# Exponentials by shifted bit patterns, PV by query halves, packed heads and free score slots in an attention and MLP kernel

## The chip, the cores and the metric

The kernel runs on one core of one Trainium2 chip. The metric is the device time of one execution in microseconds; lower is better. A run of a one-core program is called fast when it lies within 1.5% of the fastest run of the same kernel; unless it is said otherwise all numbers are from fast runs. A profile is of one execution and its span is some 2 us shorter than that execution's time. The clock that is given beside a run is TensorE's granted clock, as a share of full speed, averaged over the run.

## The reference

```python
# A: attention over 2048 tokens, 32 heads of 16;  B: token-mixing MLP with 1376 hidden units
xn = layernorm(x)                                   # x: [1, 2048, 512], bf16
q, k, v = split(xn @ wqkv)                          # 32 heads, Dh = 16
p = softmax(q @ k.T * 16 ** -0.5)                   # [32, 2048, 2048]: 134 million exponentials
A = concat(p @ v) @ wo
B = (gelu(layernorm(xn).T @ w1 + b1) @ w2 + b2).T
return x + A + B
```

## The kernel before

Scores (Q times K) are made transposed, keys on partitions; PV is the product of their exponentials with V. TensorE's results land in PSUM (`ps` in the profile), of which the kernel uses eight banks. One unit of work n is 128 keys by 512 queries of two heads, a tile of 128x1024; there are 1024 of them. Two score matmuls with 32 contracted rows each fill the tile's two PSUM banks. Three pairs of banks are score slots; one bank collects PV, one serves all else (projections, the MLP, the out-projection). A matmul is written for a split of TensorE's array, its tiling mode: score matmuls use 32 rows by 128 columns (32*128 in the profile), PV uses 128 rows by 32 columns (128*32), a column tile, and up to four column tiles work side by side (in the trace four PV matmuls of 128x512 start within 0.03 us of each other at 221.79 us, and the next four matmuls at 222.01). A scheduler written in Python goes through the program at build time with its own guesses of durations and fixes the order on every engine.

ScalarE turns most tiles into `exp` with one instruction. VectorE does some of them, with integer arithmetic on bf16 bit patterns, in five instructions. Score tiles go to the slot `n % 3`.

```python
def pslot(n):
    return n % 2 if n < 2 * NKT else n % 3

def exp_specs(n):                                   # ScalarE
    ... e.activation(pT[:, pbuf[n], :], ps[:, s_ * 1024:(s_ + 1) * 1024], ACTF.Exp, scale=LN2_128)

def d_specs(n, buf):                                # VectorE
    dW_i = max(ps + IBIAS, 0)                       # from PSUM; int16 that is read as bf16
    dM_i = (dW_i & 0x7f) | 0x3f80                   # the mantissa
    dA_i = dW_i & -128                              # the exponent alone
    dM   = dM * dM
    dM   = dW * dM                                  # exp ~ V.dW + V.dA + (171/1024 V).dM
    # (written here as formulas; each line is one VectorE instruction)

def pv_specs(item, first, last):
    for i in range(2):                              # two heads, two of four column tiles
        r = 2 * (n % 2) + i
        ... e.matmul(bank(PV_BANK)[32 * r:32 * r + 32, :], lhsT=vt[:, off:off + 32],
                     rhs=tile[:, buf, 512 * i:512 * (i + 1)], tile_position=(0, 32 * r))
# ... cut: the two head pairs' PV steps are emitted together when both are ready
# a tile goes to VectorE when the last one was 4 tiles ago and its backlog is under 1.6 us
```

V carries a column of 0.5, so that PV also gives the softmax's denominators. The head outputs stand in PSUM at 16 of each 32 rows, and the out-projection contracts 128 such rows of which half are empty (`wo_pad` holds zeros there): eight steps for each output tile.

The softmax here doesn't subtract the row's maximum and nothing guards it: scores larger than these inputs give would overflow.

## Time and profile before

| | before |
|---|---|
| time, median of the first 3 runs | 812.09 us (810.02 to 819.36) |
| ScalarE exponentials | 824 |
| VectorE exponentials | 200 |
| mean granted TensorE clock | 0.978 |

The first line is the page's busy time by engine (us, share of the span, instructions). PE is TensorE, PEld its weight loads, DVE VectorE, ACT ScalarE, POOL GpSimd.

```profile
PE 754.5 (93%) x8184; PEld 230.1 (28%) x8184; DVE 764.3 (94%) x1304; ACT 771.7 (95%) x845; POOL 76.8 (9%) x88
```

The windows view gives busy us of each engine in stretches of the span, then the granted TensorE clock as a share of full speed.

```profile
core 0: us, PE busy (x) PEld busy (x) DVE busy (x) ACT busy (x) POOL busy (x), PEclk, DMA share, GB/s
200.00:300.00 100.00, 99.11 (x1136) 27.67 (x1128) 97.95 (x164) 99.83 (x114) 0.00 (x0) 1.00 0.23 48
300.00:400.00 100.00, 97.03 (x898) 26.24 (x894) 92.27 (x153) 99.56 (x109) 0.00 (x0) 0.98 0.11 25
400.00:500.00 100.00, 94.82 (x998) 27.31 (x998) 96.31 (x161) 98.78 (x108) 0.00 (x0) 0.99 0.12 29
500.00:600.00 100.00, 91.00 (x708) 25.93 (x704) 99.11 (x166) 99.26 (x109) 0.00 (x0) 1.00 0.06 11
600.00:700.00 100.00, 95.62 (x998) 27.61 (x994) 96.38 (x162) 100.00 (x110) 0.00 (x0) 1.00 0.12 29
```

Three engines are full at once in the long middle part, and GpSimd does nothing there. So no single engine can be relieved by giving its work to another of the three.

The costliest groups of instructions: source line, engine, output and input, shapes, count, busy us and mean ns, idle time before them.

```profile
L606 ACT ACTIVATE pT<-ps 128x1024 bf16<-128x1024 f32 x824 | 763.2, 1113 | 15.4 <-PE ps L590 14.6
...
L617 DVE TENSOR_SCALAR dW<-ps 128x1024 int16<-128x1024 f32 x200 | 243.4, 1217 | 23.0 <-PE ps L590 21.9
...
L506 POOL TENSOR_SCALAR VM<-V 128x544 bf16<-128x544 bf16 x16 | 29.0, 1811 | 47.6 <-DVE V L739 42.1
```

A mean duration is no cost: successive instructions overlap (VectorE's pass over PSUM below lasts 1.23 us, and the next one starts after 1.14). What one costs an engine that is full is the step from its start to the next start. In VectorE's timeline (start us, duration us):

```profile
400.92 1.23 DVE L617 TENSOR_SCALAR dW<-ps 128x1024 int16<-128x1024 f32 x1 [1.01 <-PE ps L590]
...
402.06 0.68 DVE L628 TENSOR_TENSOR dM<-dW,dM 128x1024 bf16<-128x1024 bf16 x1
...
402.66 0.42 DVE L620 TENSOR_SCALAR dM<-dW 128x1024 int16<-128x1024 int16 x1
...
402.99 0.42 DVE L623 TENSOR_SCALAR dA<-dW 128x1024 int16<-128x1024 int16 x1
...
403.33 0.68 DVE L626 TENSOR_TENSOR dM<-dM 128x1024 bf16<-128x1024 bf16 x1
...
403.93 0.24 DVE L835 RECIPROCAL rcomp<-dcomp 128x16 f32<-128x16 f32 x1
```

The steps are 1.14, 0.60, 0.33, 0.34 and 0.60 us, together 3.01 us for one exponential. For ScalarE the chain of waits has a piece of 18 in a row, 16.61 / 18 = 0.923 us each:

```profile
402.43 16.61 ACT pT L606 x18
```

824 x 0.923 = 761 us: nearly all that ScalarE does.

### The profile page before, as it was taken

The page shows a single profiled execution, that of the slowest core. Times are in us where ns is not written, and L with a number is a line of the kernel's source. Part 1 is how long each engine was busy: PE and PEld are TensorE (multiplying, and loading weights), DVE is VectorE, ACT ScalarE, POOL GpSimd, SP SyncE. Part 2 cuts the span into 40 slices and gives each one's busy share as a digit, 9 for nine tenths or more (in the row PEclk, how much of TensorE's full clock was granted, in tenths as well). Part 3 has the DMA queues.
Part 4 walks back from the last instruction along what each step waited for, and adds up shares of the span by engine and source line. Part 5 has one row for each costly group of instructions (what it writes and reads, how often), then busy time and mean ns, then how long its engine had stood idle before and what let it go on. Part 6 is the DMA issues. An engine that isn't in the chain of part 4 may idle for free.

```text
span 813.6 us, 19375 instructions
## 1 busy us (share of the span) xinstructions
PE 754.5 (93%) x8184; PEld 230.1 (28%) x8184; DVE 764.3 (94%) x1304; ACT 771.7 (95%) x845; POOL 76.8 (9%) x88
## 2 busy tenths in 40 slices
PE   5988999999999999999999999899899999999995
PEld 3532333233222222222222222222222222222221
DVE  6879999999999988999899999999999999799985
ACT  4998999999999999999999999999999999899991
POOL 5579432000000000000000000000000000000000
PEclk9999999999999999999899999999999999799998
DMA  6040000222221212100001111000001111010010
GB/s 181 2 80 15 10 16 3 42 43 58 60 55 33 46 36 50 32 22 15 4 8 37 33 48 23 16 8 6 11 8 32 40 38 34 7 27 9 8 26 27
DMA packets 73239, 25.38 MB, mean 31 GB/s; under 512 B 63104, under 2 KB 71168, under 8 KB 73152
## 3 DMA queue, kind: packets, MB, share of 16 engines
q1 hardware_dynamic: 69984, 22.57, 12.5%
q10 hardware_dynamic: 3168, 1.57, 0.7%
q8 instruction: 64, 1.05, 0.5%
q14 instruction: 23, 0.19, 0.1%
HBM read 19.54 MB, written 2.35 MB: 27 GB/s over the span
## 4 chain that ended last, share of the span: by engine, by line
ACT 43%; DVE 31%; PE 24%; DMA 1%; issue 1%; SPq 0%; DVEq 0%
ACT pT L606 42%; DVE dW L617 10%; PE ps L590 9%; PE ps L652 7%; PE ps L681 7%; DVE dM L626 5%; DVE dM L628 4%; DVE dM L620 3%; DVE dA L623 2%; DVE OT L829 1%; DVE V L739 1%; DVE KT L720 1%; DMA x_sb<-in_A_x_dram 1%; DVE oT L844 1%; PE ps L478 0%
## 5 line engine op out<-in xcount | busy, mean ns | idle before, releaser
L606 ACT ACTIVATE pT<-ps 128x1024 bf16<-128x1024 f32 x824 | 763.2, 1113 | 15.4 <-PE ps L590 14.6
L590 PE MATMUL ps<-QT,KT 32*128 32x512 bf16 x2048 | 331.5, 390 | 23.3 <-ACT pT L606 10.7
L652 PE MATMUL ps<-pT,V 128*32 128x512 bf16 x1648 | 259.0, 393 | 7.2 <-DVE OT L829 3.3
L617 DVE TENSOR_SCALAR dW<-ps 128x1024 int16<-128x1024 f32 x200 | 243.4, 1217 | 23.0 <-PE ps L590 21.9
L590 PEld LDWEIGHTS ps<-QT,KT 32*128 32x128 bf16 x2048 | 85.1, 91 | 314.1 <-ACT pT L606 121.5
L628 DVE TENSOR_TENSOR dM<-dW,dM 128x1024 bf16<-128x1024 bf16 x200 | 137.0, 685 | 1.7
L626 DVE TENSOR_TENSOR dM<-dM 128x1024 bf16<-128x1024 bf16 x200 | 137.6, 688 | 0.0
L652 PEld LDWEIGHTS ps<-pT,V 128*32 128x32 bf16 x1648 | 62.6, 94 | 99.4 <-issue 69.6
L620 DVE TENSOR_SCALAR dM<-dW 128x1024 int16<-128x1024 int16 x200 | 86.5, 433 | 1.6
L652 PE MATMUL ps<-dW,V 128*32 128x512 bf16 x400 | 79.0, 393 | 7.2 <-DVE OT L829 7.1
L623 DVE TENSOR_SCALAR dA<-dW 128x1024 int16<-128x1024 int16 x200 | 85.0, 425 | 0.0
L652 PE MATMUL ps<-dM,VM 128*32 128x512 bf16 x400 | 77.0, 389 | 1.7 <-POOL VM L506 1.3
L652 PE MATMUL ps<-dA,V 128*32 128x512 bf16 x400 | 77.6, 391 | 0.1
L681 PE MATMUL ps<-hx,wblk 128*32 128x512 bf16 x688 | 56.0, 382 | 0.0
L681 PE MATMUL ps<-wo_pad,oT 128*32 128x512 bf16 x480 | 40.0, 382 | 0.0
L681 PE MATMUL ps<-wkv_raw,wblk 128*32 128x512 bf16 x512 | 39.2, 382 | 0.2 <-DVE osb L816 0.2
L506 POOL TENSOR_SCALAR VM<-V 128x544 bf16<-128x544 bf16 x16 | 29.0, 1811 | 47.6 <-DVE V L739 42.1
L652 PEld LDWEIGHTS ps<-dW,V 128*32 128x32 bf16 x400 | 19.3, 94 | 36.4 <-issue 21.5
L453 POOL TENSOR_SCALAR hx<-hx,mv 128x512 bf16<-128x512 bf16 x16 | 26.7, 1686 | 0.1
L652 PEld LDWEIGHTS ps<-dM,VM 128*32 128x32 bf16 x400 | 19.1, 94 | 23.9 <-issue 10.7
L652 PEld LDWEIGHTS ps<-dA,V 128*32 128x32 bf16 x400 | 19.4, 95 | 20.7 <-issue 9.7
L829 DVE COPY OT<-ps 128x512 f32<-128x512 f32 x31 | 21.2, 683 | 1.1 <-PE ps L652 0.7
(79 smaller groups left out, 353.7 us busy)
## 6 DMA issues: line engine op xcount, KB each, us to landing
wblk<-in_B_w_dram SPq DMA_DIRECT2D x10, 512.0 KB, 4.5
wblk<-in_B_w_dram SPq DMA_DIRECT2D x16, 320.0 KB, 3.5
denb<-rden_scratch SPq DMA_DIRECT2D x124, 32.0 KB, 1.9
out_dram<-osb SPq DMA_DIRECT2D x16, 128.0 KB, 1.7
dcomp<-OT SPq DMA_DIRECT2D x124, 2.0 KB, 1.7
QT<-Qall SPq DMA_DIRECT2D x120, 16.0 KB, 1.8
x_sb<-in_A_x_dram SPq DMA_DIRECT2D x3, 512.0 KB, 10.3
wkv_raw<-in_A_wqkv_dram ACTq DMA_DIRECT2D x2, 384.0 KB, 8.7
```

The lines of the kernel that those rows point to most:

```text
L453: sc.add("pool", lambda e: e.tensor_scalar(xn_sb[:, t, :], xn_sb[:, t, :], mv[:, t, 3:4], None, ALU.mult), reads=[("xn", t), ("mv", t)], w ...
L506: sc.add("pool", lambda e: e.tensor_scalar(vm_kh[:, t0_:t0_ + n, 8 * T:8 * T + 8, :], v17_kh[:, t0_:t0_ + n, 8 * T:8 * T + 8, :], CM, None ...
L590: specs.append(dict(eng="pe", fn=lambda e, r=r, bk=bk: e.matmul(bank(bk), lhsT=KT[32 * r:32 * r + 32, T, 128 * kt:128 * (kt + 1)], rhs=QT[ ...
L606: return [dict(eng="act", fn=lambda e: e.activation(pT[:, pbuf[n], :], ps[:, s_ * 1024:(s_ + 1) * 1024], ACTF.Exp, scale=LN2_128), reads=[ ...
L617: yield dict(eng="dve", fn=lambda e: e.tensor_scalar(dW_i[:, buf, :], ps[:, s_ * 1024:(s_ + 1) * 1024], IBIAS, 0.0, ALU.add, ALU.max), rea ...
L620: yield dict(eng="dve", fn=lambda e: e.tensor_scalar(dM_i[:, buf, :], dW_i[:, buf, :], 0x7f, 0x3f80, ALU.bitwise_and, ALU.bitwise_or), rea ...
L623: yield dict(eng="dve", fn=lambda e: e.tensor_scalar(dA_i[:, buf, :], dW_i[:, buf, :], -128, None, ALU.bitwise_and), reads=[("dW", buf)], ...
L626: yield dict(eng="dve", fn=lambda e: e.tensor_tensor(dM[:, buf, :], dM[:, buf, :], dM[:, buf, :], ALU.mult), reads=[("dM", buf)], writes=[ ...
L628: yield dict(eng="dve", fn=lambda e: e.tensor_tensor(dM[:, buf, :], dW[:, buf, :], dM[:, buf, :], ALU.mult), reads=[("dW", buf), ("dM", bu ...
L652: specs.append(dict(eng="pe", fn=lambda e, r=r, off=off, i=i: e.matmul(bank(PV_BANK)[32 * r:32 * r + 32, :], lhsT=vt[:, off:off + 32], rhs ...
L681: specs.append(dict(eng="pe", fn=lambda e, c=c, w=w: e.matmul(bank(EX_BANK)[32 * c:32 * c + w, :], lhsT=lhs_of(32 * c, 32 * c + w), rhs=rh ...
L829: yield "pvev", [dict(eng="dve", fn=lambda e: e.tensor_copy(OT32[:, eb, :], bank(PV_BANK)), reads=[("bank", PV_BANK)], writes=[("OT32", eb)])]
```

## The change

The intent is to move exponentials from ScalarE to VectorE, by making VectorE's cheaper, and to give TensorE room for the extra PV terms.

1. The VectorE exponential is now a sum of four piecewise-linear powers of two: the bit pattern W and three copies with an integer added (22, 58, 94). Three passes of SBUF to SBUF replace four, none of them with two inputs, and GpSimd takes about a third of them.
2. One PV step covers one head pair in four column tiles, two heads by two halves of 256 queries, so it never needs a partner.
3. The heads are packed by DMA, so the out-projection needs four steps in place of eight, and the final product goes to GpSimd.
4. A score tile goes to the slot that comes free first; ScalarE or VectorE takes any tile that is ready.
5. GpSimd's single-scalar instructions get a second scalar of 1.0.

```diff
-CM = 171.0 / 1024.0
-KAPPA = 2.16705
+SHIFTS = (22, 58, 94)
+CM = 13.0 / 16.0
+KAPPA = 5.0415723
-NPB = 10
-NDB = 3
+NPB = 20
+NXB = 8                       # x_sb is reused for probability buffers
@@ VectorE exponential (dm, dA, dm2, dM removed)
+        def shift_spec(eng, w, o, k):
+            return dict(eng=eng, fn=lambda e: e.tensor_scalar(
+                buf_i(o), buf_i(w), float(SHIFTS[k]), 1.0, ALU.add, ALU.mult), ...
+                cost=(SH_I, SH_L) if eng == "pool" else (TS_I, TS_L))
@@ PV
-            for i in range(2):
-                r = 2 * (n % 2) + i
-                    bank(PV_BANK)[32 * r:32 * r + 32, :], ... rhs=tile[:, buf, 512 * i:512 * (i + 1)]
+            for c in range(4):
+                h, i = divmod(c, 2)
+                    bank(PV_BANK)[32 * c:32 * c + 32, 256 * par:256 * par + 256], ...
+                    rhs=buf(p, 512 * i + 256 * h, 512 * i + 256 * h + 256)
@@ epilogue: 8 DMAs of 16x256 pack each block's heads; product on GpSimd
-            yield "dve", [dict(eng="dve", fn=lambda e: e.tensor_tensor(oT[:, qb % 2, G, :], OT32[...], denb[...], ALU.mult)
+            yield "pool", [dict(eng="pool", fn=lambda e, cs=cs: e.tensor_tensor(oT[0:m, qb % 2, T, cs], oC32[...], denb[...], ALU.mult)
@@ slots
-            s_ = pslot(n)
+                s_ = min(free_slots, key=slot_time)
@@ which tile goes to VectorE
-                if n - last_d >= D_GAP and n % BN <= D_LAST and free_d and backlog <= D_BACKLOG:
+            if ready_q and fly < D_FLY and len(free_p) >= 4 + P_KEEP:      # and backlog(t) <= D_BACK = 0.5
@@ ... cut: the scheduler keeps GpSimd's instructions apart in time from some of VectorE's; reloading x for the residual, the tail
```

## The prediction

> **What bounds the kernel now.** In the windows view, 200 to 700 us, ScalarE is busy 98.8 to 100%, VectorE 92 to 99%, TensorE 91 to 99%: three engines are full together. ScalarE does 824 of the 1024 exponentials of 128x1024. The chain of waits runs 18 of them in 16.61 us (402 to 419 us), 0.923 us each, so 761 of ScalarE's 772 busy us. Its other 42 us are mostly prologue (18 us idle before 160 us) and tail (17 us in the last 34). VectorE does 200 exponentials in five instructions; start to start in the timeline 1.14 + 0.33 + 0.34 + 0.60 + 0.60 = 3.01 us, so 602 us, plus about 160 us of other work. TensorE pays about 0.33 us for a score run with its change of tiling mode, 0.33 us for the first step of another run, 0.22 us per further step. When only one head pair of a PV step is ready, two of four column tiles work.
>
> **What the change does (counts from the built program's instruction order).**
> - Exponentials: VectorE 200 -> 266, ScalarE 824 -> 758.
> - A VectorE exponential is one 1.14 us PSUM pass and three integer shifts (798: 527 on VectorE at 0.335 us, the trace's step for the int16 tensor_scalar, 271 on GpSimd). VectorE: 266 x 1.14 + 527 x 0.335 = 480 us instead of 602; the oT product (31 x 0.60) leaves too. Load about 620 us.
> - GpSimd: no trace has this shift. [...] The trace's one-scalar form takes 1.65 us for 544 elements, so this rests on the second scalar. [...] The shifts fit under the PSUM pass.
> - PV: 1424 two-tile steps of 512 columns become 1822 four-tile steps of 256. The trace's four-tile matmuls of 128 columns step at 56 ns per group, so 107 ns for 256 is safe.
> - Out-projection: 480 -> 240 matmuls, 13 us less.
> - Score runs 771 -> 636, others 769 -> 634: 270 mode changes of 0.11 us go. TensorE, estimated: 636 x 0.33 + 634 x 0.11 + 1475 x 0.215 = 597 us, plus score pairs that don't coincide: clear of saturation.
> - 248 DMAs of 16 KB are added, off the path.
>
> **On the critical path.** VectorE loses about 140 us, TensorE gets slack, so ScalarE alone binds: 66 x 0.923 = 61 us less, 812 - 61 = 751. I add 4 us for ScalarE idling where the static order misjudges GpSimd or clock-throttled stretches (at 400 us matmuls step at half speed).
>
> **Predicted: 755 us, range 742 to 779.** Faster by over 2%: 0.94, within 2%: 0.04, slower: 0.02.
>
> **Would show it right.** ScalarE about 706 us busy, still 98% between 200 and 700 us; exp interval 0.92 us; VectorE at 80 to 88% of the span, GpSimd about 40%; shifts of 0.42 us (VectorE) and about 1.05 us (GpSimd); TensorE at or under 90%; the chain's ScalarE share up from 43% to over 60%.
>
> **Would make it wrong.** GpSimd shifts of 1.5 us or more, or VectorE shifts stretched behind GpSimd, so PV waits for late shift buffers and score slots stay full; a granted clock that falls because four column tiles now work; ScalarE idle above 60 us because scores come late; a longer tail from the DMA packing.

Cut from the GpSimd item are its estimate of one shift and a reason for contention with VectorE, as no trace or run shows what they rested on. The estimate came to 1.07 us a shift, 290 us for 271; of its two terms only 0.19 us was read from a trace, and it is "this" in "this rests on the second scalar". "The shifts fit under the PSUM pass", "about 1.05 us" and "about 40%" for GpSimd were forecasts that came of it; the result below measures them.

## The result

| | before | changed |
|---|---|---|
| median time | 811.48 us (4 runs, 810.02 to 819.36) | 752.63 us (4 runs, 750.77 to 753.34) |
| exponentials, ScalarE / VectorE | 824 / 200 | 758 / 266 |
| mean granted clock in the profile | 0.978 | 0.968 |

The ratio is 0.924 (95% interval 0.919 to 0.929). A ratio is the mean time of one kernel's fast runs over that of the other's of the same rounds, so it isn't quite the ratio of the medians. The page's first line, then windows and groups of the changed kernel:

```profile
PE 691.1 (92%) x12388; PEld 306.2 (41%) x12388; DVE 644.6 (86%) x1061; ACT 710.8 (95%) x779; POOL 351.5 (47%) x391
```

```profile
core 0: us, PE busy (x) PEld busy (x) DVE busy (x) ACT busy (x) POOL busy (x), PEclk, DMA share, GB/s
200.00:300.00 100.00, 96.95 (x1758) 43.11 (x1754) 88.94 (x140) 100.00 (x113) 39.55 (x39) 1.00 0.25 57
300.00:400.00 100.00, 92.14 (x1586) 39.06 (x1582) 89.99 (x146) 99.25 (x109) 47.83 (x48) 0.98 0.13 31
400.00:500.00 100.00, 95.17 (x1646) 39.40 (x1644) 92.17 (x147) 100.00 (x110) 47.71 (x49) 0.98 0.18 43
500.00:600.00 100.00, 91.97 (x1546) 38.14 (x1544) 85.32 (x137) 95.11 (x104) 48.66 (x48) 0.91 0.11 25
600.00:700.00 100.00, 94.92 (x1660) 40.83 (x1656) 90.94 (x145) 97.81 (x108) 50.00 (x49) 0.97 0.17 40
```

```profile
L640 ACT ACTIVATE pT<-ps 128x1024 bf16<-128x1024 f32 x529 | 527.2, 1142 | 10.4 <-PE ps L616 9.7
...
L651 DVE TENSOR_SCALAR pT<-ps 128x1024 int16<-128x1024 f32 x197 | 240.4, 1220 | 42.7 <-PE ps L616 41.4
...
L656 POOL TENSOR_SCALAR pT<-pT 128x1024 int16<-128x1024 int16 x137 | 143.5, 1047 | 175.6 <-DVE pT L656 125.1
```

ScalarE is still full, VectorE is not. ScalarE's busy time fell by 771.7 - 710.8 = 60.9 us and the profiled span by 813.6 - 750.4 = 63.2 us; what ScalarE leaves idle in the span went from 41.9 to 39.6 us. (By its span, the profiled execution of the kernel before was longer than the median one; the medians differ by 58.9 us.) One exponential still costs ScalarE 0.92 us: the chain of waits has four in 3.68 us.

```profile
700.85 3.68 ACT x_sb L640 x4
```

In the timeline GpSimd's shift (1.05 us) lies under VectorE's PSUM pass (1.23 us), which leaves VectorE 1.14 + 2 x 0.335 us for this exponential:

```profile
402.77 1.05 POOL L656 TENSOR_SCALAR pT<-pT 128x1024 int16<-128x1024 int16 x1 [0.62 <-DVE pT L656]
402.83 1.23 DVE L651 TENSOR_SCALAR x_sb<-ps 128x1024 int16<-128x1024 f32 x1
...
403.97 0.42 DVE L656 TENSOR_SCALAR pT<-pT 128x1024 int16<-128x1024 int16 x1
...
404.31 0.42 DVE L656 TENSOR_SCALAR pT<-x_sb 128x1024 int16<-128x1024 int16 x1
...
404.64 1.22 DVE L651 TENSOR_SCALAR pT<-ps 128x1024 int16<-128x1024 f32 x1
```

### The profile page after: what moved, and what is told of

It is laid out like the page before. It is cut to its first block, busy times and chain, and to the rows that moved or that the text cites. A ratio compares the mean times of both kernels' runs of the same rounds, so it can differ in the third digit from the quotient of the medians.

```text
span 750.4 us, 28208 instructions
## 1 busy us (share of the span) xinstructions
PE 691.1 (92%) x12388; PEld 306.2 (41%) x12388; DVE 644.6 (86%) x1061; ACT 710.8 (95%) x779; POOL 351.5 (47%) x391
## 4 chain that ended last, share of the span: by engine, by line
ACT 41%; PE 31%; DVE 20%; POOL 3%; issue 2%; SPq 2%; DMA 0%; DVEq 0%; POOLq 0%
ACT pT L640 29%; PE ps L679 13%; ACT x_sb L640 12%; PE ps L616 11%; DVE pT L651 7%; PE ps L709 7%; DVE pT L656 5%; DVE x_sb L651 3%; SPq L371 2%; DVE OT L863 2%; DVE x_sb L656 1%; POOL pT L656 1%; POOL x_sb L656 1%; PE ps L758 1%; DVE denb L928 0%
## 5 line engine op out<-in xcount | busy, mean ns | idle before, releaser
L640 ACT ACTIVATE pT<-ps 128x1024 bf16<-128x1024 f32 x529 | 527.2, 1142 | 10.4 <-PE ps L616 9.7
L651 DVE TENSOR_SCALAR pT<-ps 128x1024 int16<-128x1024 f32 x197 | 240.4, 1220 | 42.7 <-PE ps L616 41.4
L679 PE MATMUL ps<-pT,V 128*32 128x256 bf16 x4456 | 243.7, 282 | 13.6 <-DVE OT L863 7.0
L640 ACT ACTIVATE x_sb<-ps 128x1024 bf16<-128x1024 f32 x229 | 248.4, 1153 | 1.9 <-PE ps L616 1.9
L656 POOL TENSOR_SCALAR pT<-pT 128x1024 int16<-128x1024 int16 x137 | 143.5, 1047 | 175.6 <-DVE pT L656 125.1
L679 PE MATMUL ps<-x_sb,V 128*32 128x256 bf16 x1768 | 117.5, 282 | 9.0 <-DVE OT L863 6.3
L656 DVE TENSOR_SCALAR pT<-pT 128x1024 int16<-128x1024 int16 x288 | 120.8, 445 | 2.6
L656 POOL TENSOR_SCALAR x_sb<-pT 128x1024 int16<-128x1024 int16 x64 | 67.0, 1046 | 66.9 <-DVE pT L656 50.1
L651 DVE TENSOR_SCALAR x_sb<-ps 128x1024 int16<-128x1024 f32 x69 | 84.2, 1220 | 16.0 <-PE ps L616 15.4
L656 POOL TENSOR_SCALAR pT<-x_sb 128x1024 int16<-128x1024 int16 x53 | 55.4, 1046 | 63.2 <-DVE pT L656 46.1
L679 PE MATMUL ps<-pT,VM 128*32 128x256 bf16 x772 | 55.6, 278 | 0.4 <-POOL VM L531 0.3
```

What stands on the lines that cost most here:

```text
L640: return [dict(eng="act", fn=lambda e: e.activation(buf(pbuf[n]), ps[:, s_ * 1024:(s_ + 1) * 1024], ACTF.Exp, scale=LN2_128), reads=[("ban ...
L651: return dict(eng="dve", fn=lambda e: e.tensor_scalar(buf_i(w), ps[:, s_ * 1024:(s_ + 1) * 1024], IBIAS, 0.0, ALU.add, ALU.max), reads=[(" ...
L656: return dict(eng=eng, fn=lambda e: e.tensor_scalar(buf_i(o), buf_i(w), float(SHIFTS[k]), 1.0, ALU.add, ALU.mult), reads=[("pT", w)], writ ...
L679: specs.append(dict(eng="pe", fn=lambda e, c=c, h=h, i=i, off=off: e.matmul(bank(PV_BANK)[32 * c:32 * c + 32, 256 * par:256 * par + 256], ...
```

## The experiments

The theory at first (A): ScalarE's count N of exponentials sets the time, 0.923 N + 53 us, where 53 us is what both kernels leave beside them (811.5 - 0.923 x 824 = 51, 752.6 - 0.923 x 758 = 53). The rival (B): TensorE's freed time is the gain. After the first four runs a third theory (C) was needed. Each group of four ran on one chip, with its own runs of the kernel before (medians 815.11, 814.80 and 815.64 us), so ratios are the safer comparison. All twelve gave correct outputs.

| run | N | 0.923 N + 53 | median us | ratio to before (95%) | clock in the profile |
|---|---|---|---|---|---|
| changed kernel | 758 | 753 | 752.63 | 0.924 (0.919 to 0.929) | 0.968 |
| e1_cap200 | 824 | 814 | 843.49 | 1.036 (1.031 to 1.040) | 0.850 |
| e2_pv_pairs | 763 | 757 | 778.87 | 0.955 (0.950 to 0.960) | 0.981 |
| e3_dve_shifts | 793 | 785 | 780.27 | 0.958 (0.951 to 0.965) | 0.961 |
| e7_old_exp | 823 | 813 | 848.44 | 1.043 (1.038 to 1.048) | 0.817 |
| e9_cap200_pairs | 824 | 814 | 836.27 | 1.027 (1.021 to 1.032) | 0.960 |
| e10_cap200_filler | 824 | 814 | 815.98 (fast runs 813.76) | 0.999 (0.994 to 1.003) | fast runs 0.966 to 0.977 |
| e6_two_shifts | 720 | 718 | 728.62 | 0.892 (0.888 to 0.897) | 0.973 |
| e8_one_shift | 717 | 715 | 721.20 | 0.884 (0.881 to 0.887) | 0.950 |
| e12_old_exp_filler | 821 | 811 | 819.63 | 1.006 (1.002 to 1.011) | 0.958 |
| e11_one_shift_filler | 720 | 718 | 716.84 | 0.879 (0.875 to 0.883) | 0.974 |
| e4_fixed_slots | 758 | 753 | 760.84 | 0.933 (0.929 to 0.938) | 0.965 |
| e5_one_scalar | 758 | 753 | 1042.12 | 1.279 (1.273 to 1.285) | 0.802 |

### e1_cap200: as many exponentials on VectorE as before

```diff
-            if ready_q and fly < D_FLY and len(free_p) >= 4 + P_KEEP:
+            if ready_q and fly < D_FLY and len(free_p) >= 4 + P_KEEP and len(on_d) < 200.0 * (next_n - BN) / (NN - BN):
```

> The changed kernel, with its VectorE exponentials held at 200 (spread evenly), as the kernel before had; ScalarE does 824. Theory A (ScalarE's count of exponentials sets the time: 0.923 us each plus the 51 to 53 us that both kernels leave beside them): 0.923 x 824 + 53 = 814 us, range 803 to 820. Theory B (TensorE's freed time sets it, through four-tile PV and fewer mode changes): all of that is still there and 198 four-tile PV groups of 0.107 us fewer, so 731 to 755 us.

Measured: 843.49 us, 3.6% slower than the kernel before. B is refuted: nothing of the gain is left. But A's 803 to 820 us is missed too. The windows show what neither theory had: the granted clock.

```profile
200.00:300.00 100.00, 95.59 (x1624) 38.89 (x1622) 74.73 (x114) 97.86 (x110) 31.17 (x31) 0.97 0.28 61
300.00:400.00 100.00, 88.45 (x1138) 30.62 (x1130) 55.86 (x89) 94.51 (x102) 29.56 (x30) 0.81 0.09 22
400.00:500.00 100.00, 93.27 (x1348) 34.37 (x1344) 58.18 (x91) 94.55 (x102) 29.61 (x30) 0.84 0.17 40
500.00:600.00 100.00, 91.67 (x1024) 29.87 (x1020) 49.59 (x80) 88.75 (x94) 27.56 (x28) 0.64 0.06 14
```

Where the clock is lowest (0.64) ScalarE is emptiest (88.75). The trace's clock records have two values only, 1.0 and 0.5, as in both kernels' traces, so 0.64 is a mixture. In TensorE's timeline the start-to-start step of a four-tile group of 256 columns is 0.21 us there:

```profile
559.63 0.43 PE L679 MATMUL ps<-pT,V 128*32 128x256 bf16 x4
559.84 0.43 PE L679 MATMUL ps<-x_sb,V 128*32 128x256 bf16 x4
```

In the changed kernel the same step is 0.11 us:

```profile
404.89 0.28 PE L679 MATMUL ps<-pT,VM 128*32 128x256 bf16 x4
...
405.00 0.28 PE L679 MATMUL ps<-pT,V 128*32 128x256 bf16 x4
```

TensorE runs at half speed there, and its busy time (91.67 of 100 us) hides this: a slow matmul is busy for longer (0.43 against 0.28 us). No wait of TensorE or its weight loads that the list has from 500 to 600 us was longer than 1.6 us, so no longer gap was needed for a clock of 0.64. Theory C: with cheap PV and few extra terms TensorE has too little to do, its clock is taken down, and at the low clock it is too slow for ScalarE.

The trace bears out the first half. Its clock changes at multiples of about 3.4 us (the stretches at the low clock in the traces of both kernels last 3.41, 6.83, 10.24 or 13.65 us, but for the last ones, 10.21 and 9.80 us, where the execution ends). Count in each 3.4 us piece the time in which columns stream through TensorE, at 0.42 ns for a column at full clock (the trace's step for 512 columns is 0.216 us). Leaving out about the first and last 50 us, the clock of e1_cap200 fell 13 times: in the pieces just before, columns streamed 43% of the time (33 to 49%). In the 138 pieces at full clock after which it stayed up it was 70%, and only 10 of these were under 50%. The changed kernel has the same picture with 5 falls (41 to 49%), against 73% in its 176 other pieces.

### e7_old_exp: everything but the new exponential

```diff
+        # in place of the shifts, on VectorE alone: dA, dm, dm2, dM as before, each a job of its own
-D_BACK = 0.5
+D_BACK = 2.5
```

> All of the change but the new exponential: five VectorE instructions as before, nothing on GpSimd, with PV by query halves, DMA packing and first-free score slots. Admission limit loosened to 2.5 us of backlog so that VectorE gets 201 exponentials, ScalarE 823. Theory A (ScalarE's count): 0.923 x 823 + 53 = 813 us, range 800 to 820, so no gain at all from PV, packing and slots by themselves. Theory B (TensorE's freed time is the gain): below 785 us.

Measured: 848.44 us, clock 0.817. B is refuted again; PV by halves, packing and free slots by themselves made it 4.3% slower. The top of A's range is missed by 28 us. Two of its windows:

```profile
300.00:400.00 100.00, 89.45 (x1064) 29.09 (x1060) 87.85 (x145) 94.43 (x102) 4.87 (x4) 0.74 0.11 27
...
500.00:600.00 100.00, 89.97 (x1012) 28.61 (x1010) 84.13 (x138) 92.14 (x98) 2.90 (x4) 0.66 0.10 23
```

### e10_cap200_filler: more work for TensorE

If C holds, useless TensorE work should make e1_cap200 faster. After two PV steps of five, four matmuls with zero weights add zero to the PV accumulator.

```diff
+        # ... cut: zt, a tile of zeros
+            fill[0] += 0.4
+            if fill[0] >= 1.0 and not first and pv_left[b] > 0 and b > 0:
+                fill[0] -= 1.0
+                for c in range(4):
+                    ... e.matmul(bank(PV_BANK)[...], lhsT=zt[:, :], rhs=buf(p, ...), start=False, stop=False, tile_position=(0, 32 * c))
```

> The run with VectorE held at 200 exponentials plus 649 groups of four matmuls with zero weights into the PV accumulator (they add zero; 649 x 0.107 = 69 us of TensorE work for nothing). Theory C: clock 0.95 or more, 808 to 825 us, faster than without the filler (843 us). Rival D: slower than 843 us or the same. If the clock depends on the values and not on the work issued, it stays near 0.85 and the time near or over 843 us.

Measured: four runs, 815.98 us in the median, one of them slow (826.55 us, and the profile fell on it). The three fast ones took 812.84, 813.76 and 818.20 us at clocks of 0.977, 0.977 and 0.966; the four runs of e1_cap200 had 0.850 to 0.869. So 69 us of useless work saved about 28 us (ratio to before 0.999 against 1.036), and A's 814 us is met. C holds, and its rival D (the 843 us came of the order of work, so more TensorE work can't help) falls. The fillers go through the scheduler, so the order of the other work moved a little too; no run held it fixed. As the weights were zeros and the clock rose all the same, work that changes no result was enough here.

### e12_old_exp_filler: the same for e7_old_exp

```diff
+            fill[0] += 0.46        # as in e10_cap200_filler
```

> The run with all of the change but the new exponential (848 us, clock 0.817), plus 657 filler groups of four zero-weight matmuls (70 us of TensorE work for nothing). 203 exponentials on VectorE, 821 on ScalarE. Theory C (that run was slow by its clock): clock 0.95 or more and 803 to 825 us, near 0.923 x 821 + 53 = 811. Rival (PV by halves, packing or slots cost 35 us by their waits or order): 848 us or more.

Measured: 819.63 us, clock 0.958, inside C's range. The same two windows:

```profile
300.00:400.00 100.00, 90.16 (x1534) 39.10 (x1528) 93.95 (x158) 95.52 (x105) 3.63 (x5) 0.93 0.12 28
...
500.00:600.00 100.00, 85.11 (x1366) 35.48 (x1358) 89.36 (x150) 93.16 (x102) 2.66 (x4) 0.90 0.08 17
```

TensorE gets through 1534 matmuls in place of 1064 and 1366 in place of 1012, in about the same busy time or less, as each takes less time; ScalarE gets through 105 and 102 instructions in place of 102 and 98. The clock fell 9 times in place of 22 (counted as above). With the clock held by filler, the parts other than the exponential gain nothing: 0.6% slower than before, the same within 2%.

### e2_pv_pairs: PV as before, all else as changed

```diff
-            for c in range(4):
-                h, i = divmod(c, 2)
+            for i in range(2):
+                r = 2 * par + i
+                    bank(PV_BANK)[32 * r:32 * r + 32, :], ... rhs=buf(p, 512 * i, 512 * i + 512), tile_position=(0, 32 * r)
@@ ... cut: packing, tail and the scheduler's pairing of PV steps, fitted to this layout
```

> The changed kernel with PV as before: two column tiles of 512 columns per step, both head pairs emitted together when both are ready; packing and tail fitted to that layout. The scheduler puts 261 exponentials on VectorE, 763 on ScalarE. Theory A (ScalarE's count alone): 0.923 x 763 + 53 = 757 us, range 750 to 764. Theory B (TensorE is a second limit, and the query halves are what took it away): 1807 two-tile steps take 194 us if all pair up and 388 us if none do, in place of 196 us; with half of them unpaired some 97 us more TensorE work, part of it in ScalarE's way: 775 us or more.

Measured: 778.87 us, in B's range and 22 us over A's 757, at a good clock (0.981). In the list of waits ScalarE waits 31.6 us in all for score matmuls, against 11.6 us in the changed kernel: 20 us more, nearly the whole 22 us. So with this many PV terms TensorE delivers scores late, and PV by query halves is needed to collect the gain. Whether the two-tile steps themselves or the order that the scheduler makes for pairs is at fault was not separated. In these windows ScalarE no longer is full:

```profile
200.00:300.00 100.00, 98.31 (x1204) 32.58 (x1192) 91.06 (x143) 94.93 (x106) 42.68 (x42) 1.00 0.23 50
300.00:400.00 100.00, 94.14 (x916) 27.95 (x914) 78.21 (x126) 93.86 (x101) 43.72 (x43) 0.93 0.13 30
```

### e9_cap200_pairs: 200 exponentials and PV as before

This joins the edits of e1_cap200 and e2_pv_pairs.

> The run with VectorE held at 200 exponentials, with PV put back to two-tile steps of 512 columns: 1624 PV steps that cost TensorE more. Theory C (with PV by halves and few exponentials on VectorE, TensorE is too often idle, its granted clock falls to 0.85 in the mean, and at the low clock it is too slow for ScalarE): the wasteful PV keeps TensorE busy, clock 0.95 or more, and the time falls from 843 to 805 to 828 us although TensorE has more to do. Rival D (843 us came of the order that the held-back scheduler makes, or of shifts and slots): more TensorE work on top, so 843 us or more.

Measured: 836.27 us, clock 0.942 to 0.960. The clock came back as C said, but the time fell by only 7 us and C's range of 805 to 828 us was missed. The wasteful PV gives the clock back (0.850 to 0.869 without it) and is in ScalarE's way at the same time, as the waits of e2_pv_pairs show (31.6 against 11.6 us). Why the kernel before, which also uses two-tile PV, does without this loss (812 us) is open; it has 200 PV steps fewer, and its scheduler was written for pairs. The filler runs and the trace, not this run, carry C.

### e3_dve_shifts: no shift on GpSimd

```diff
-                pl.append((est([sp_]), 1, "shp", (j, sp_), SH_I))
+                pass
-                    sh_jobs.append(dict(n=n, w=w, o=o, k=k, ok=lambda k=k: k > 0))
+                    sh_jobs.append(dict(n=n, w=w, o=o, k=k, ok=lambda k=k: True))
```

> The changed kernel with all shifts on VectorE, none on GpSimd. The scheduler then puts 231 exponentials on VectorE (693 shifts), 793 on ScalarE. Theory A (ScalarE's count): 0.923 x 793 + 53 = 785 us, range 776 to 792. Rival (GpSimd's shifts cost VectorE what they save, since some VectorE shifts took up to 1.06 us beside them): the same as with GpSimd, 745 to 762 us.

Measured: 780.27 us; A's 785 us is met and the rival is refuted. GpSimd's part is worth 28 us, by way of 35 exponentials that VectorE has room for.

### e4_fixed_slots: slots in rotation

```diff
-                s_ = min(free_slots, key=slot_time)
+                s_ = next_n % 3        # and only when that slot is free
@@ ... cut: the scheduler's look ahead at the next two slots follows the rotation
```

> The changed kernel with score slots in fixed rotation (tile number modulo 3), not the slot that came free first. 266 and 758 exponentials as in the changed kernel. If the free choice matters: ScalarE idles when the slot in turn is still held by VectorE's 1.14 us pass, 760 to 790 us. If only ScalarE's count matters: 750 to 757 us.

Measured: 760.84 us (759.03 to 762.88), just inside the first range. The free choice of slots is worth about 8 us here (ratio to before 0.933 against 0.924; the two were timed in different sessions and their intervals just overlap, so its size is not sharp). Nor is its cause: from 300 to 400 us the clock is 0.88 and ScalarE is busy 90.81 us, against 0.98 and 99.25 in the changed kernel, so the 8 us may be a low clock as well as the slots.

### e5_one_scalar: GpSimd's shift without the second scalar

```diff
-                buf_i(o), buf_i(w), float(SHIFTS[k]), 1.0, ALU.add, ALU.mult),
+                buf_i(o), buf_i(w), float(SHIFTS[k]), None, ALU.add),        # GpSimd only
```

> The changed kernel with GpSimd's shifts in the one-scalar form (add alone, no multiplication by 1.0); same values, same order of instructions. In the trace of the kernel before, the one-scalar form takes 1.57 us for 512 and 1.65 us for 544 elements, so my estimate for 1024 is 2.5 to 3.1 us in place of 1.05. 271 of them are then 680 to 840 us: GpSimd becomes the limit and the time is 780 to 900 us. If the form does not matter for int16: shifts of 1.05 us and 750 to 756 us.

Measured: 1042.12 us, more than the 900 us that I gave. The size of the shift was right (2.77 us, minimum/median/maximum in ns), the effect of it was not:

```profile
L656 POOL TENSOR_SCALAR pT<-pT x137: 2768/2769/3187, 62.8 to 1025.3; 128x1024 int16<-128x1024 int16 x137
...
L656 DVE TENSOR_SCALAR pT<-x_sb x103: 378/426/1253, 101.4 to 1017.6; 128x1024 int16<-128x1024 int16 x103
```

GpSimd is busy for 827 of 1045 us, so it is no plain limit either, though it is now the largest part of the chain that ended last (47%). The order is fixed at build time for shifts of 1.02 us; with 2.77 us PV waits for GpSimd (the list of waits has TensorE's weight loads waiting for it 162 us in total at one group alone), then scores and ScalarE wait, and the clock falls to 0.80 as well. How much each of these costs was not separated.

### e6_two_shifts and e8_one_shift: fewer terms

ScalarE's count is what pays, so VectorE's exponential should be as short as accuracy allows. A fit of the weighted sum to 2^x over one octave gives a largest relative error of 0.24% for three shifts, 0.40% for two and 0.78% for one.

```diff
-SHIFTS = (22, 58, 94)
-CM = 13.0 / 16.0
-KAPPA = 5.0415723
+SHIFTS = (42, 88)                      # e8_one_shift: (64,)
+CM = 0.75                              # e8_one_shift: 0.6875
+KAPPA = 3.6041321889671325             # e8_one_shift: 2.052487086692896, and either engine may take the shift
```

> The changed kernel with two shifts in place of three (shifts 42 and 88, last weight 0.75; the fit's largest error goes from 0.24 to 0.40%, near bf16 rounding). The scheduler puts 304 exponentials on VectorE, 720 on ScalarE. Theory A with a good clock: 0.923 x 720 + 53 = 718 us, range 710 to 728. By my estimate of TensorE's full-clock work (583 us of 718, 81%, against 79% in the changed kernel, whose clock is 0.968) the clock stays at 0.95 or more. A rival limit (VectorE, GpSimd at 319 shifts, or score slots) would show as over 730 us.

> The changed kernel with one shift (64, weight 0.6875; largest error of the fit 0.78%), which either engine may take. 307 exponentials on VectorE, 717 on ScalarE, so theory A with a good clock gives 0.923 x 717 + 53 = 715 us. TensorE's full-clock work is about 551 us, 77% of that. Theory C: less busy than the changed kernel's 79%, so the clock drops to 0.90 to 0.96 and the time is 718 to 735 us, no better than two shifts in spite of less work on three engines. Rival (only ScalarE's count matters): 708 to 718 us.

Measured: 728.62 us for two shifts, just over A's range of 710 to 728; in the stretch from 200 to 300 us ScalarE is busy only 88.5 us at a full clock. The list of waits says why: of the 11.5 us idle it waited 7.7 us for VectorE's part of the MLP's activation (ga_sb), once for 5.9 us. One shift gives 721.20 us at a clock of 0.950, inside C's range and outside the rival's. Both are faster than the changed kernel. TensorE's full-clock work in the two texts is an estimate of mine: 79% agrees with the prediction's 597 us of 752.63, and 583 and 551 us differ by 301 PV steps of 0.107 us. The clocks were 0.968, 0.973 and 0.950 for three, two and one shift.

### e11_one_shift_filler: one shift, with the clock held

```diff
+            fill[0] += 0.2         # on e8_one_shift
```

> The one-shift kernel (721 us, clock 0.95 with a stretch at 0.82) plus 265 filler groups (28 us of TensorE work). 304 exponentials on VectorE, 720 on ScalarE: 0.923 x 720 + 53 = 718. Theory C: clock 0.965 or more; the gain from it is bounded by the 10 us that ScalarE idles more in the low-clock stretches, so 710 to 720 us. Rival (TensorE's own work is near the limit at this speed, so filler costs): 722 to 735 us.

Measured: 716.84 us, clock 0.974 in the profile and up to 0.991 in the timed runs. In the stretch from 400 to 500 us e8_one_shift had this line:

```profile
400.00:500.00 100.00, 94.08 (x1266) 32.38 (x1266) 81.97 (x106) 94.02 (x101) 8.15 (x9) 0.82 0.16 36
```

With the filler the same stretch, with more matmuls, has ScalarE full:

```profile
400.00:500.00 100.00, 95.02 (x1569) 38.53 (x1566) 89.96 (x116) 99.53 (x110) 6.54 (x8) 1.00 0.18 42
```

That stretch is the best for the filler. From 200 to 300 us ScalarE is busier without it (97.68 against 93.54 us), and from 300 to 400 us too (98.89 against 96.49, at a clock of 0.98 against 0.90); the two profiled spans are equal, 717.8 us without and 717.6 us with it. By its median this is the fastest version, 12.1% under the kernel before. Its gain over e8_one_shift (ratios 0.879 and 0.884, intervals 0.875 to 0.883 and 0.881 to 0.887) is not clear of noise, so whether the filler helps here is not shown.

## Why the prediction was right, and where its steps were not

- **The time, 755 us against 752.63, and its main term: right.** 66 exponentials left ScalarE, at 0.923 us each 61 us; ScalarE's busy time fell by 60.9 us. The 4 us that were added for ScalarE's idling were not needed: its idle time fell by 2 us. e3_dve_shifts, with a different count and a good clock, lies within 5 us of the same line; e6_two_shifts, e12_old_exp_filler and e2_pv_pairs lie 11, 9 and 22 us above it, so the count is not everything.
- **VectorE's exponential: right.** 1.14 us and steps of 0.335 us stayed; the busy share is 86% (80 to 88% was said).
- **GpSimd's shift: right in size, not in its grounds.** 1.07 us was said and 1.046 us measured, but no trace or run shows the larger term of that estimate. That it needs the second scalar was an inference; e5_one_scalar shows it (2.77 us without). In bf16 the 128x544 instruction took 1.81 us with one scalar before and 0.67 us with two after (means). VectorE's shifts had a median of 0.42 us, and each of the 38 of 527 that took over 0.55 us (up to 1.06 us) overlaps an instruction of GpSimd, by 0.28 to 0.78 us; of the other 489, 429 overlap none and 51 by less than 0.09 us. Why a shift takes longer under such an overlap was not shown. e3_dve_shifts shows that GpSimd's help pays nevertheless. GpSimd's share was 47%, not 40%: the estimate counted only the shifts (284 us measured) and left out some 68 us of other work.
- **"TensorE gets slack, so ScalarE alone binds": right for this kernel, in part by luck, wrong as a rule.** The prediction had no term for what slack does to the clock. With 200 exponentials on VectorE the same TensorE code leaves slack, its clock falls to 0.85, and the time is 30 us over the line (843.49 against 814). The changed kernel escapes, as I read it, because its own 266 exponentials bring 4 PV terms each, which keep TensorE occupied (1822 PV steps in place of 1624; the clock fell 5 times in place of 13). A sign of it is in the changed kernel: from 500 to 600 us the clock is 0.91 and ScalarE is busy 95.11 us, below the predicted 98%, which the mean from 200 to 700 us still meets (98.4%). Undoing the count alone costs 91 us (843.49 - 752.63), not 61.
- **"A granted clock that falls because four column tiles now work": the wrong sign.** In e1_cap200 the clock fell after pieces in which columns streamed 33 to 49% of the time, in the changed kernel after 41 to 49%, and useless work in four column tiles raised it: 0.850 to 0.869 in e1_cap200, 0.966 to 0.977 with filler, and 0.817 to 0.958 from e7_old_exp to e12_old_exp_filler.
- **TensorE at or under 90%: wrong, 92%.** Busy time counts a four-tile group for 0.28 us though the next starts after 0.11 us, and it counts slow stretches too, so it doesn't measure room. The mode changes did fall as counted (771 to 636 runs of score matmuls in the traces); one costs about 0.11 us (in both traces a step of 0.32 to 0.33 in place of 0.22 us). Why it does was not shown.
- **ScalarE's share of the chain over 60%: wrong, 41% (43% before).** The chain goes back through whatever released each step. As I read it, ScalarE frees one of three slots, which lets TensorE make the score that ScalarE needs, so the chain passes through TensorE although ScalarE is full; this was not tested. The windows view answers what the chain did not.
- **The tail: right.** After the last exponential 16.7 us remained before (796.9 to 813.6) and 17.5 us now (732.9 to 750.4).
- **What each part is worth.** The exponential with GpSimd's help supplies the gain; PV by halves is needed to collect it (22 us over the line without it); free slots, or the better clock beside them, give about 8 us. The DMA packing and the shorter out-projection were only tried together with other parts, so their share is open.

## What to carry to other kernels

When three engines are full, price a change by what it takes off the engine that stays full, at its start-to-start step, and check that no other engine becomes the limit. Then look at the granted clock too: here an optimisation of TensorE was a loss when nothing filled the time it freed (ratios 1.036 and 1.043), and the proof is a run with useless matmuls added (0.999 and 1.006). An order that is fixed at build time is only as good as its durations: measure each instruction form, above all on GpSimd (1.046 us with two scalars, 2.77 us with one), before scheduling with it.
